# Moving the gelu derivatives of the first two chunks to fixed places in the order of a speech-joint kernel

## The chip, the cores and the metric

The kernel runs on one core of a Trainium2 chip. The metric is the device time of one execution in microseconds: the median of several runs for a verdict, and the hardware profiler's record of one execution for the reasons. The engines are TensorE (PE), VectorE (DVE), ScalarE (ACT), GpSimd (POOL) and SyncE (SP, used here for DMA issues only).

## The reference

Two strided convolutions, each followed by a tanh-gelu, feed a joint network; the kernel computes its output and all gradients.

```python
h = gelu(sum(xp[:, i:i+T] @ w1[i] for i in range(3)))[:, ::2]
f = gelu(sum(hp[:, i:i+T1] @ w2[i] for i in range(3)))[:, ::2]
j = tanh((f @ w_f)[:, :, None, :] + (g @ w_g)[:, None, :, :])
out = einsum("btud,dv->btuv", j, w_o)
```

x is (2, 16000, 256), g is (2, 8, 256), out is (2, 4000, 8, 256), everything in bfloat16. The eight results are `out` and the gradients of x, w1, w2, g, w_f, w_g and w_o for a given `grad_out`. The backward pass needs the derivative of each gelu at each position; that derivative work is what the change moves.

## The kernel before

**Tiling.** The 2 x 4000 output positions lie on one axis of 8016 columns (16 between the batches), cut into 16 chunks of 512 columns. A chunk's first convolution gives two tiles (even and odd positions, `par` 0 and 1) of 256 channels, its second convolution one. Channels lie on the 128 partitions in two halves, so a tile is 128x1024 elements.

**Stages of a chunk.** `conv_units` does the first convolution: PE writes `ps` (one of seven PSUM buffers), ACT copies it to `g_x`, `gelu` makes HT of it. `conv2_units` does the second one and its gelu gives FT. `fe_units` multiplies FT by w_f and ACT writes FE. `tanh` (ACT) makes JT for each of eight u. `joint_units` handles a pair of u: two products of grad_out with w_o's transpose (`gj`), evicted by DVE as NGZ with JSQ, the square of JT, as an operand; the output blocks (`o_block`, evicted by ACT); and the products for w_o's gradient (`gwo`, from JR, which is JT transposed). POOL adds the NGZ of all u into ACCN and the last time into NGFE. The backward pass of a chunk (`d1_units` makes GF from NGFE and G2; `row_units` turns tiles into rows; `d5_units` makes GH from GF and G1; then weight gradients and the gradient of x) runs during the next chunk's iteration.

**The gelu** (L248 on, called for each convolution tile) returns two lists of operations. `first`: ACT's Square into g_sq, a DVE scalar_tensor_tensor into g_s, ACT's Sigmoid in g_s, a DVE product into HT or FT. `second` is the derivative: five DVE operations, two tensor_scalar and three tensor_tensor, that end in G1 or G2. A chunk has three gelus. For chunk 0 each list is cut in two halves of 512 columns. The derivatives reuse the scratch tiles g_x, g_sq and g_s, which are free again only after them. Scratch comes from `gel` (three buffers of each name); for chunk 0's second convolution it comes from `rowp`, a pool of six tiles which `row_units` and `ghr_units` use later.

**The order.** The outer loop is over chunks. Iteration n weaves the joint of chunk n (the main generator) with a fill chain: the convolutions of chunk n + 1 and the backward pass of chunk n - 1. The main generator of chunk 0 yields 16 steps for each of four pairs of u, 64 in all (four `gj`, four transposes for JR, then output blocks and gwo); later chunks have 48. After each main step `weave` takes up to two operations from `later` (the `first` lists), one from `late` (the `second` lists) if it is open, and then a unit of the fill chain as often as a ratio allows: 0.4 for chunk 0 and 0.92 later. `late` opens when `conv2_units` of the next chunk has handed in its lists. Instructions are traced in this order, but the framework's scheduler then orders every engine's queue: an instruction traced late may be queued early if its operands are ready. `tc.keep_in_program_order` pins an instruction behind what was traced before it. Derivatives of chunks 2 and later are pinned (`pinned`), those of chunks 0 and 1 are not. In the profile the derivatives of chunks 0 and 1 carry L265, those of later chunks L268.

**Ahead of the loop** chunk 0's convolutions run with `warm` between them: matmuls on a zero tile `idle`, which is taken from the x pool (`xcp`, six tiles, four for a chunk).

Of the kernel before, what the change touches and what calls it, by code (L numbers as in the profile page):

```python
# [13 lines left out]
BF16 = mybir.dt.bfloat16  # L14
FP32 = mybir.dt.float32
ALU = mybir.AluOpType
# [4 lines left out]
GELU_A = float(2.0 * np.sqrt(2.0 / np.pi))  # L21

P = 128
KT = 2
# [4 lines left out]
CW = 512  # L29
# [3 lines left out]
def kernel(  # L33
# [22 lines left out]
    nc = tc.nc  # L56
    B, T, _ = x.shape
# [6 lines left out]
    def geom(n):  # L64
        c0 = n * CW
        return c0, min(CW, L - c0)
# [35 lines left out]
    xcp = pool("xcp", 6)  # L102
# [10 lines left out]
    rowp = pool("rowp", 6)  # L113
# [13 lines left out]
    def ps_f32():  # L127
        return psp.tile([P, 512], FP32, name="ps", tag="ps")
# [117 lines left out]
    def scratch(name, spare):  # L246
        if spare:
            return rowp.tile([P, 8, P], BF16, name="rows")[:].rearrange("p (k a) b -> p k (a b)", k=KT)  # L248
        return gel.tile([P, KT, CW], BF16, name=name)


    later, late = deque(), deque()
    late_open = [False]
    held = []
    NOSYNC = mybir.DependencyInfo(mybir.DependencyClass.NoSync, mybir.DependencyReason.DATA)

    def pump(k):
        for _ in range(k):
            if later:
                later.popleft()()  # L260

    def pump_late(k):
        for _ in range(k):
            if late and late_open[0]:
                late.popleft()()  # L265

    def pinned(op, n):
        return op if n <= 1 else (lambda: tc.keep_in_program_order(op()))  # L268

    def gelu(xb, W, h, gp, off, kts=((0, KT),), spare=False):  # L270

        sq, s = scratch("g_sq", spare), scratch("g_s", spare)
        TT, TS, STT = nc.vector.tensor_tensor, nc.vector.tensor_scalar, nc.vector.scalar_tensor_tensor
        first, second = [], []
        for (k0, k1) in kts:
            sq_, s_, x_ = sq[:, k0:k1, :W], s[:, k0:k1, :W], xb[:, k0:k1, :W]
            h_, gp_ = h[:, k0:k1, off:off + W], gp[:, k0:k1, off:off + W]
            first += [
                partial(nc.scalar.activation, out=sq_, in_=x_, func=ACT.Square, scale=GELU_R),
                partial(STT, out=s_, in0=sq_, scalar=1.0, in1=x_, op0=ALU.add, op1=ALU.mult),  # L280
                partial(nc.scalar.activation, out=s_, in_=s_, func=ACT.Sigmoid, scale=GELU_A),
                partial(TT, out=h_, in0=s_, in1=x_, op=ALU.mult),
            ]
            second += [
                partial(TS, out=sq_, in0=sq_, scalar1=3.0 * GELU_A, scalar2=GELU_A, op0=ALU.mult, op1=ALU.add),
                partial(TS, out=x_, in0=s_, scalar1=-1.0, scalar2=1.0, op0=ALU.mult, op1=ALU.add),
                partial(TT, out=sq_, in0=sq_, in1=x_, op=ALU.mult),
                partial(TT, out=sq_, in0=sq_, in1=h_, op=ALU.mult),
                partial(TT, out=gp_, in0=sq_, in1=s_, op=ALU.add),
            ]  # L290
        return first, second


    HALVES = ((0, 1), (1, 2))

    seconds0 = []
# [41 lines left out]
    def conv2_units(n):  # L338
        c0, W = geom(n)
        st = S[n]  # L340
        HT = st["HT"]
        if n > 0:
            pump(len(later))
        FT = ftp.tile([P, KT, CW], BF16, name="FT")
        G2 = ftp.tile([P, KT, CW], BF16, name="G2")
        st["FT"], st["G2"] = FT, G2
        if W % P:
            nc.gpsimd.memset(FT[:, :, W:W // P * P + P], 0.0)
        xb = scratch("g_x", n == 0)
        for mt in range(KT):  # L350
            ps = ps_f32()
            k = 0
            for (i, par, off) in ((1, 0, 2), (0, 1, 1), (2, 1, 2)):
                for kt in range(KT):
                    nc.tensor.matmul(ps[:, :W], lhsT=W2[:, i, kt, mt * P:(mt + 1) * P],  # L355
                                     rhs=HT[:, par, kt, off:off + W], start=(k == 0), stop=(k == 5))
                    k += 1
            nc.scalar.copy(out=xb[:, mt, :W], in_=ps[:, :W])
            yield
        first, second = gelu(xb, W, FT, G2, 0, HALVES if n == 0 else ((0, KT),), n == 0)  # L360
        if n == 0:
            for f in first:
                f()
        else:
            later.extend(first)
        late.extend(pinned(f, n) for f in second + seconds0)
        seconds0.clear()
        late_open[0] = True

    def fe_units(n):  # L370
        c0, W = geom(n)
        if n > 0:
            pump(len(later))
        FE = fep.tile([P, KT, CW], FP32, name="FE")
        S[n]["FE"] = FE
        for mt in range(KT):
            ps = ps_f32()
            for kt in range(KT):
                nc.tensor.matmul(ps[:, :W], lhsT=WF[:, kt, mt * P:(mt + 1) * P], rhs=S[n]["FT"][:, kt, :W],
                                 start=(kt == 0), stop=(kt == KT - 1))  # L380
            nc.scalar.copy(out=FE[:, mt, :W], in_=ps[:, :W])
            yield
# [351 lines left out]
    def chain(*gens):  # L734
        for gen in gens:
            yield from gen

    def empty(k):
        for _ in range(k):
            yield  # L740

    def weave(main, fill, ratio):

        due = 0.0
        for _ in main:
            pump(2)
            pump_late(1)
            due += ratio
            while due >= 1.0:
                due -= 1.0  # L750
                if next(fill, StopIteration) is StopIteration:
                    due = -1e9
# [7 lines left out]
    nc.sync.dma_start(out=W2[:], in_=w2.rearrange("i (kt p) n -> p i kt n", p=P))  # L760
    nc.sync.dma_start(out=WF[:], in_=w_f.rearrange("(kt p) n -> p kt n", p=P))
    nc.sync.dma_start(out=WO[:], in_=w_o.rearrange("(kt p) n -> p kt n", p=P))
    idle = xcp.tile([P, KT, CW + 16], BF16, name="XC")
    nc.vector.memset(idle[:], 0.0)
    small = const.tile([P, 1], FP32, name="small")
    nc.vector.memset(small[:], 0.0)
    nc.scalar.activation(out=small[:], in_=small[:], func=ACT.Sigmoid)
# [1 line left out]
    def warm(k):  # L769

        ps = ps_f32()
        for _ in range(k):
            tc.keep_in_program_order(nc.tensor.matmul(ps[:], lhsT=idle[:, 0, 0:P], rhs=idle[:, 0, 0:CW],
                                                      start=True, stop=True))
        yield

# [47 lines left out]
    for n in range(G):  # L824
        back, fwd = n > 0, n + 1 < G
        conv = conv_units(n + 1) if fwd else iter(())
        conv2 = conv2_units(n + 1) if fwd else iter(())
        late_open[0] = False
        parts = []
        if back:  # L830
            d1, e, rows, ghr = d1_units(n - 1), e_units(n - 1), row_units(n - 1), ghr_units(n - 1)
            parts += [islice(conv, 2), islice(d1, 1), islice(conv, 1), d1, conv, alternate(rows, d5_units(n - 1)),
                      gwf_units(n - 1), gw2_units(n - 1), islice(ghr, 1), islice(conv2, 1), ghr, conv2, islice(e, 6)]
            if fwd:
                parts.append(fe_units(n + 1))
            parts.append(e)
        else:
            parts += [conv, empty(3), islice(conv2, 1), empty(3), conv2, empty(3), fe_units(n + 1)]
        fill = chain(*parts)
        ratio = (0.92 if n > 0 else 0.4) if n + 1 < G else 0.72  # L840
        for up in range(U // 2):
            step = n * (U // 2) + up
            for i in range(2):
                if 2 * step + 4 + i < len(order):
                    load_got(*order[2 * step + 4 + i])
            if step + 1 < len(orderp):
                load_go(*orderp[step + 1])
            if up == 1:
                load_fr(n)
            if back and up < 2:  # L850
                load_xr(n - 1, 2 * up)
                load_xr(n - 1, 2 * up + 1)
            main = joint_units(n, up)
            weave(main, fill, ratio)
            if up == U // 2 - 1:
                for _ in fill:
                    pump(2)
                    pump_late(1)
                pump(len(later))
                late_open[0] = True  # L860
                pump_late(len(late))
            for i in range(2):
                if 2 * step + 2 + i < len(order):
                    tanh(*order[2 * step + 2 + i])
            if step + 1 < len(orderp):
                load_jr(*orderp[step + 1])
            if n + 2 < G:
                load_x(n + 2, ((0, 1, 3, 2)[up],))
    n = G - 1
# [30 lines left out]
    for b in range(B):  # L900
# [11 lines left out]
        for dt in range(KT):  # L912
            nc.tensor.matmul(GWG_ps[:, dt * D:(dt + 1) * D], lhsT=GR8[:, b, dt * P:(dt + 1) * P],
                             rhs=ngR[:].rearrange("u kt p -> u (kt p)"),
# [34 lines left out]
```

## Time and profile before

| what | value |
|---|---|
| median of the runs | 850.34 us (848.83 to 851.24, three runs) |
| profiled execution | 843.12 us |
| its span | 841.4 us |
| PE busy | 812.8 us (97%), mean granted clock 0.994 |
| DVE busy | 620.3 us (74%) |
| ACT busy | 678.4 us (81%) |
| POOL busy | 394.6 us (47%) |
| start (before FE of chunk 0) | 0 to 27.17 us |
| iteration of chunk 0 | 27.17 to 70.65 us |
| iteration of chunk 1 | 70.65 to 121.6 us |
| DMA moved | 187.21 MB, mean 223 GB/s |

The profiled execution is the record of one run, and its span is what lies between the first and the last instruction. A group's mean mixes contended and free executions: a 128x1024 tensor_scalar at L265 took 0.43 us at 38.9 us and 2.35 us at 49.29 us.

### The profile page before, as it was taken

What the parts mean: (1) busy time and instruction counts of PE and PEld (TensorE: products, weight loads), DVE (VectorE), ACT (ScalarE), POOL (GpSimd) and SP (SyncE); (2) the same over time, 40 slices, a digit from 0 to 9 for tenths busy, and PEclk for the clock granted to TensorE, in tenths of its full rate; (3) what the DMA queues carried; (4) which work ended last, traced back from release to release, by engine and by line L of the source; (5) the groups of instructions that cost most, each with busy time, mean ns of one, the idle gap of its engine ahead of it and who ended that gap; (6) DMA issues with size and microseconds to landing.
All of it is one profiled execution on the core that took longest, in us unless ns stands there. A gap on an engine that the chain in (4) does not pass through costs nothing.

```text
span 841.4 us, 17055 instructions
## 1 busy us (share of the span) xinstructions
PE 812.8 (97%) x6396; PEld 598.2 (71%) x6396; DVE 620.3 (74%) x1217; ACT 678.4 (81%) x1080; POOL 394.6 (47%) x423
## 2 busy tenths in 40 slices
PE   7969999999999999999999999999999999999997
PEld 3546677767768677676766777677686776878796
DVE  4896696876778767697866968768687676967644
ACT  3889998796978969699796987969789696987744
POOL 1154544444534535444486644445345354445661
PEclk9999999999999999999999999999999999999999
DMA  9988999999999999999999999999999999999954
GB/s 188 194 198 182 212 229 233 216 251 235 225 221 259 226 229 245 243 222 183 224 255 210 233 233 228 251 210 265 238 237 264 210 227 231 220 210 228 243 157 135
DMA packets 398515, 187.21 MB, mean 223 GB/s; under 512 B 346464, under 2 KB 382200, under 8 KB 398432
## 3 DMA queue, kind: packets, MB, share of 16 engines
q1 hardware_dynamic: 378112, 119.00, 77.9%
q0 software_dynamic: 20320, 67.12, 27.5%
q8 instruction: 50, 0.82, 0.4%
q14 instruction: 33, 0.27, 0.1%
HBM read 51.38 MB, written 50.34 MB: 121 GB/s over the span
## 4 chain that ended last, share of the span: by engine, by line
PE 43%; ACT 41%; DVE 6%; issue 5%; DMA 4%; POOL 0%; SPq 0%; ACTq 0%; POOLq 0%; DVEq 0%
ACT JT L396 12%; PE ps L593 7%; ACT OUT L692 6%; ACT JSQ L617 6%; PE GWO_ps L729 6%; PE ps L580 6%; PE ps L690 6%; ACT rows L462 5%; PE ps L355 5%; PE ps L524 4%; PE ps L623 4%; ACT g_s L260 3%; ACT g_x L323 3%; PE pst L460 2%; ACT GX L583 2%
## 5 line engine op out<-in xcount | busy, mean ns | idle before, releaser
L646 POOL TENSOR_TENSOR ACCN<-ACCN,NGZ 128x1024 f32<-128x1024 f32 (+1 forms) x80 | 168.7, 2109 | 69.1 <-DVE NGZ L627 68.0
L627 DVE SCALAR_TENSOR_TENSOR NGZ<-JSQ,ps 128x512 bf16<-128x512 bf16 (+3 forms) x272 | 167.5, 640 | 43.2 <-PE ps L623 39.9
L692 ACT CAST OUT<-ps 128x512 bf16<-128x512 f32 (+1 forms) x252 | 148.4, 600 | 58.4 <-PE ps L690 58.2
L396 ACT ACTIVATE JT<-FE,GE 128x512 bf16<-128x512 f32 (+3 forms) x272 | 182.3, 711 | 4.0 <-PE ps L623 1.9
L617 ACT ACTIVATE JSQ<-JT 128x1024 bf16<-128x1024 bf16 (+1 forms) x128 | 135.8, 1064 | 25.6 <-DVE NGZ L627 25.6
L729 PE MATMUL GWO_ps<-GO,JR 128*128 128x256 bf16 (+1 forms) x1008 | 148.6, 273 | 2.1 <-DVE JR L462 2.1
L690 PE MATMUL ps<-WO,JT 128*128 128x256 bf16 (+1 forms) x1008 | 148.7, 274 | 0.3 <-ACT rows L462 0.3
L717 POOL DMA_DIRECT2D out_dram<-OUT x76 | 55.8, 735 | 184.4 <-ACT OUT L692 171.5
L623 PE MATMUL ps<-GOT,WOT 128*128 128x512 bf16 (+1 forms) x512 | 139.2, 376 | 0.8 <-DVE rows L462 0.8
L260 DVE SCALAR_TENSOR_TENSOR g_s<-g_sq,g_x 128x1024 bf16<-128x1024 bf16 (+2 forms) x49 | 81.2, 1657 | 50.1 <-ACT g_sq L260 50.1
L729 PEld LDWEIGHTS <-JR 128*128 128x128 bf16 (+1 forms) x1008 | 96.9, 98 | 28.6 <-DVE JR L462 2.4
L690 PEld LDWEIGHTS <-JT 128*128 128x128 bf16 (+1 forms) x1008 | 97.9, 98 | 22.1 <-issue 1.6
L580 PE MATMUL ps<-W1T,GH 128*128 128x256 bf16 (+2 forms) x756 | 100.4, 273 | 0.0
L408 DVE TENSOR_TENSOR ACC<-ACC,ps 128x512 f32<-128x512 f32 x90 | 61.5, 684 | 44.5 <-PE ps L524 32.8
L580 PEld LDWEIGHTS <-GH 128*128 128x128 bf16 (+2 forms) x756 | 83.5, 116 | 13.0
L320 PE MATMUL ps<-XC,W 128*128 128x512 bf16 (+1 forms) x384 | 91.3, 375 | 1.1 <-DMA XC<-in_x_dram 1.1
L593 PE MATMUL ps<-rows,XR 128*128 128x256 bf16 (+1 forms) x756 | 90.4, 273 | 0.0
L593 PEld LDWEIGHTS <-XR 128*128 128x128 bf16 (+1 forms) x756 | 74.0, 98 | 11.6
L583 ACT CAST GX<-ps 128x512 bf16<-128x512 f32 (+2 forms) x126 | 72.2, 587 | 10.5 <-DMA out_dram<-GX 4.1
L241 POOL DMA_DIRECT2D out_dram<-GX x67 | 36.7, 548 | 82.1 <-ACT GX L583 75.0
L623 PEld LDWEIGHTS <-WOT 128*128 128x128 bf16 x512 | 48.5, 98 | 33.6 <-issue 2.3
L320 PEld LDWEIGHTS <-W 128*128 128x128 bf16 x384 | 37.4, 98 | 38.5 <-issue 1.4
(131 smaller groups left out, 1214.2 us busy)
## 6 DMA issues: line engine op xcount, KB each, us to landing
GO<-in_grad_out_dram SPq DMA_DIRECT2D x56, 512.0 KB, 5.3
out_dram<-OUT POOLq DMA_DIRECT2D x56, 512.0 KB, 5.5
out_dram<-GX POOLq DMA_DIRECT2D x55, 256.0 KB, 4.3
XR<-in_x_dram POOLq DMA_DIRECT2D x39, 256.0 KB, 6.3
XR<-in_x_dram POOLq DMA_DIRECT2D x13, 320.0 KB, 6.2
GOT<-in_grad_out_dram SPq DMA_TRANSPOSE x136, 5.7
JR<-JT SPq DMA_TRANSPOSE x128, 4.8
GO<-in_grad_out_dram SPq DMA_DIRECT2D x4, 384.0 KB, 5.0
```

Source lines behind the costliest of these rows:

```text
L260: later.popleft()()
L320: nc.tensor.matmul(ps[:, :W], lhsT=W1[:, i, kt, mt * P:(mt + 1) * P], rhs=st["X", c][:, kt, 16 + sh:16 + sh + W], start=(k == 0), stop=(k ...
L396: nc.scalar.activation(out=JT[:, mt, lo:hi], in_=S[n]["FE"][:, mt, lo:hi], func=ACT.Tanh, bias=GE[:, b, mt, u:u + 1], scale=1.0)
L580: nc.tensor.matmul(ps[:M, cj * D:(cj + 1) * D], lhsT=GH[:, par, kt, o:o + s * (M - 1) + 1:s], rhs=W1T[:, i, kt, :], start=(j == 0), stop=( ...
L593: nc.tensor.matmul(ps[:, dt * D:(dt + 1) * D], lhsT=XR[:M, 4 * k + i + 2 * (1 - par), dt * P:(dt + 1) * P], rhs=t[:M, g + 2 * par:g + 2 * ...
L617: nc.scalar.activation(out=JSQ[:, :, :W], in_=JT[:, :, :W], func=ACT.Square)
L623: nc.tensor.matmul(ps[:, :W], lhsT=WOT[:, kt, mt * P:(mt + 1) * P], rhs=GOT[:, kt, :W], start=(kt == 0), stop=(kt == KT - 1))
L627: nc.vector.scalar_tensor_tensor(out=NGZ[:, mt, lo:hi], in0=JSQ[:, mt, lo:hi], scalar=1.0, in1=ps[:, lo:hi], op0=ALU.subtract, op1=ALU.mul ...
L646: st["last"] = nc.gpsimd.tensor_tensor(out=out, in0=in0, in1=st["NGZ", u][:, :, :W], op=ALU.add)
L690: nc.tensor.matmul(ps[:M, j * V:(j + 1) * V], lhsT=st["JT", u][:, kt, o:o + M], rhs=WO[:, kt, :], start=(kt == 0), stop=(kt == KT - 1))
L692: nc.scalar.copy(out=OUT[:M, k, :], in_=ps[:M, :])
L729: nc.tensor.matmul(GWO_ps[:, dt, :], lhsT=JR[:M, j, dt, k, :], rhs=GO[:M, k, j * V:(j + 1) * V], start=(n_gwo[0] == 0), stop=(n_gwo[0] == ...
```

## The change

- A third queue, `slow`, with a budget `slow_open` that begins at 5. `weave` takes at most one operation from it at each main step while the budget lasts (`pump_slow`). Derivatives of chunks 0 and 1 go there, in the order first convolution (both parities), then second convolution; later chunks use `late` as before.
- `pinned` pins every derivative, also those of chunks 0 and 1.
- Derivatives of chunk 0 are whole (128x1024) and no longer in halves: 15 operations in place of 30. With chunk 1's 16 (one is a POOL copy) `slow` holds 31: five are taken in the first steps of chunk 0's iteration; `opened(15)`, placed in the fill chain one unit after chunk 1's second convolution, allows 15 more; the last 11 are taken in the first steps of chunk 1's iteration.
- The scratch of chunk 1's second convolution also comes from the row tiles.
- `idle` is taken from the row tiles, not from the x pool.

```diff
-    later, late = deque(), deque()
-    late_open = [False]
+    later, late, slow = deque(), deque(), deque()
+    late_open, slow_open = [False], [5]
...
+    def pump_slow(k):
+        for _ in range(min(k, slow_open[0], len(slow))):
+            slow_open[0] -= 1
+            slow.popleft()()
+
     def pinned(op, n):
-        return op if n <= 1 else (lambda: tc.keep_in_program_order(op()))
+        return lambda: tc.keep_in_program_order(op())
...
-            second += [
-                partial(TS, out=sq_, in0=sq_, scalar1=3.0 * GELU_A, scalar2=GELU_A, op0=ALU.mult, op1=ALU.add),
...
-            ]
+        sq_, s_, x_, h_, gp_ = sq[:, :, :W], s[:, :, :W], xb[:, :, :W], h[:, :, off:off + W], gp[:, :, off:off + W]
+        second += [
+            partial(TS, out=sq_, in0=sq_, scalar1=3.0 * GELU_A, scalar2=GELU_A, op0=ALU.mult, op1=ALU.add),
+            partial(TS, out=x_, in0=s_, scalar1=-1.0, scalar2=1.0, op0=ALU.mult, op1=ALU.add),
+            partial(TT, out=sq_, in0=sq_, in1=x_, op=ALU.mult),
+            partial(TT, out=sq_, in0=sq_, in1=h_, op=ALU.mult),
+            partial(TT, out=gp_, in0=sq_, in1=s_, op=ALU.add),
+        ]
...
-        xb = scratch("g_x", n == 0)
+        xb = scratch("g_x", n <= 1)
...
-        first, second = gelu(xb, W, FT, G2, 0, HALVES if n == 0 else ((0, KT),), n == 0)
+        first, second = gelu(xb, W, FT, G2, 0, HALVES if n == 0 else ((0, KT),), n <= 1)
...
-        late.extend(pinned(f, n) for f in second + seconds0)
+        (late if n > 1 else slow).extend(pinned(f, n) for f in (second + seconds0 if n > 1 else seconds0 + second))
         seconds0.clear()
-        late_open[0] = True
+        late_open[0] = n > 1
...
+    rate = [1]
+
+    def opened(k):
+        slow_open[0] += k
+        return
+        yield
...
             pump_late(1)
+            pump_slow(rate[0])
...
-    idle = xcp.tile([P, KT, CW + 16], BF16, name="XC")
-    nc.vector.memset(idle[:], 0.0)
+    idle = rowp.tile([P, 8, P], BF16, name="rows")[:].rearrange("p a b -> p (a b)")
+    nc.vector.memset(idle, 0.0)
...
-            parts += [conv, empty(3), islice(conv2, 1), empty(3), conv2, empty(3), fe_units(n + 1)]
+            parts += [conv, empty(3), islice(conv2, 1), empty(3), conv2, empty(1), opened(15), empty(2), fe_units(n + 1)]
...
                 pump_late(len(late))
+                if n == 0:
+                    pump_slow(len(slow))
+                    slow_open[0] = len(slow)
```

More of the change, by code (lines that the diff above doesn't have):

```diff
@@ L283, in gelu @@
             ]
-            second += [
-                partial(TS, out=sq_, in0=sq_, scalar1=3.0 * GELU_A, scalar2=GELU_A, op0=ALU.mult, op1=ALU.add),
[L286 to L289, printed above, removed]
-            ]
+        sq_, s_, x_, h_, gp_ = sq[:, :, :W], s[:, :, :W], xb[:, :, :W], h[:, :, off:off + W], gp[:, :, off:off + W]
[6 more added lines that the diff above has]
+        ]
         return first, second
@@ L772, in warm @@
         for _ in range(k):
-            tc.keep_in_program_order(nc.tensor.matmul(ps[:], lhsT=idle[:, 0, 0:P], rhs=idle[:, 0, 0:CW],
+            tc.keep_in_program_order(nc.tensor.matmul(ps[:], lhsT=idle[:, 0:P], rhs=idle[:, 0:CW],
                                                       start=True, stop=True))
```

## The prediction

> **What bounds the kernel now.** I read first the busy time of each engine by stretch: the start (to 27.17), chunk 0's iteration (to 70.65), the first half of the next one, and for comparison a whole steady iteration. Columns: the stretch, its length, busy time with instruction count for PE, PE's weight loads, DVE, ACT, POOL, then PE's granted clock, DMA share, GB/s.
>
> ```profile
> 27.17:70.65 43.48, 36.05 (x253) 22.43 (x252) 38.31 (x81) 37.83 (x58) 16.62 (x12) 0.92 0.80 181
> 70.65:92.00 21.35, 20.80 (x150) 13.01 (x147) 14.41 (x28) 20.78 (x32) 13.62 (x17) 1.00 1.06 221
> ...
> 121.60:172.30 50.70, 50.05 (x396) 36.95 (x394) 38.27 (x70) 42.34 (x67) 23.11 (x24) 1.00 1.12 236
> ```
>
> From 70.65 on PE is at 97 to 99% and at full clock: what PE loses after that is lost for good. Only chunk 0's iteration has slack: PE idles 7.4 of 43.5 us and part of the rest runs at a low clock, while DVE (38.3) and ACT (37.8) are nearly full. The second view is the order of work there, on DVE, then ACT and PE (start, duration, engine, line, operation, tiles, idle time before with what ended it).
>
> ```profile
> 36.49 2.37 DVE L260 SCALAR_TENSOR_TENSOR g_s<-g_sq,g_x 128x1024 bf16<-128x1024 bf16 x1
> ...
> 48.61 0.76 DVE L265 TENSOR_SCALAR g_sq<-g_sq 128x1024 bf16<-128x1024 bf16 x1
> 49.29 2.35 DVE L265 TENSOR_SCALAR g_x<-g_s 128x1024 bf16<-128x1024 bf16 x1
> 51.67 0.69 DVE L265 TENSOR_TENSOR g_sq<-g_sq,g_x 128x1024 bf16<-128x1024 bf16 x1
> ...
> 56.83 2.23 DVE L260 SCALAR_TENSOR_TENSOR g_s<-g_sq,g_x 128x1024 bf16<-128x1024 bf16 x1
> ...
> 61.25 0.68 DVE L260 TENSOR_TENSOR FT<-g_s,g_x 128x1024 bf16<-128x1024 bf16 x1
> ...
> 66.54 0.69 DVE L627 SCALAR_TENSOR_TENSOR NGZ<-JSQ,ps 128x512 bf16<-128x512 bf16 x1 [1.98 <-PE ps L623]
> ```
>
> ```profile
> 53.56 1.08 ACT L260 ACTIVATE g_sq<-g_x 128x1024 bf16<-128x1024 bf16 x1
> ```
>
> ```profile
> 54.21 0.38 PE L460 MATMUL pst<-ident,JT 128*128 128x128 bf16 x4 [1.55 <-DVE JR L462]
> ...
> 59.45 1.05 PE L729 MATMUL GWO_ps<-GO,JR 128*128 128x256 bf16 x8 [2.13 <-DVE JR L462]
> 61.98 1.01 PE L379 MATMUL ps<-FT,WF 128*128 128x512 bf16 x2 [1.48 <-DVE FT L260]
> ```
>
> Derivative work (L265) sits ahead of the second chunk's second gelu: its square is ready at 54.64, its next DVE step starts at 56.83. FT comes at 61.93 and PE waits for DVE three times, 5.2 us. After it PE runs slowly:
>
> ```profile
> 60.00:62.00 2.00, 0.52 (x6) 0.31 (x4) 1.97 (x3) 1.71 (x3) 1.04 (x1) 0.60 0.13 34
> 62.00:64.00 2.00, 2.00 (x7) 0.97 (x7) 1.90 (x4) 0.71 (x2) 0.00 (x0) 0.50 0.68 237
> 64.00:66.00 2.00, 2.00 (x8) 1.03 (x7) 0.56 (x1) 1.46 (x3) 0.00 (x0) 0.50 0.00 0
> ```
>
> Half clock (0.50) from about 61 to 67: some 3 us of PE work.
>
> **Part 1, the start.** Before, 30 half-size derivatives of chunk 0 run between 13.0 and 30.8 us; 22 begin before 27.8, mostly while DVE has nothing else. Three of them stand in the queue before the last HT piece (0.29 + 0.54 = 0.83 us in the chain of waits). Taking them out gives at most 0.83, but ACT is busy without a gap from 11.04 to 17.38 and fixes that piece too: between -0.8 and 0. The idle tile leaves the XC buffers, so one x load needs no release; PE's wait for XC at 31.44 is 1.08 us: between -1.1 and 0. I take -0.6 for both. What is lost: these 30 (12 x 0.29 + 18 x 0.41 = 10.9 us) cost almost nothing there, and now lie in later stretches.
>
> **Part 2, five pinned operations in steps 1 to 5 of chunk 0's iteration.** Full-size spacing from the rows: scalar form 0.46, tensor form 0.73, so one set of five is 2 x 0.46 + 3 x 0.73 = 3.1 us. They now stand between the NGZ evictions and the first JR copies, and behind them the g_s step of 36.49. NGZ begins about 32.0; 4 x 0.61 + 4 x 0.35 + 3.1 ends near 38.5, so g_s starts 2 us later; it took 2.37 because POOL's add ran beside it (1.22 in the next one), so it ends at 39.7 against 38.86. ACT, full from 27.8 to 54.64 but for 0.75 us, waits for it: +0.8 (bounds 0 and +2).
>
> **Part 3, up to FT.** Chunk 1's ten derivatives ahead of 54.6 (2.9 + 5.2 = 8.1 us, port waits in them) go. They are worth little up to the square at 54.64, which ACT's full queue sets (54.64 + 0.8 - 0.6 = 54.84). From there: g_s 2.2, sigmoid 1.06, product 0.68: FT at 58.8, 3.1 earlier than 61.93.
>
> **Part 4, fifteen pinned operations in steps 38 to 52.** The fill is served in steps 3, 5, 8, 10, 13 and 15 of each sixteen, which puts the release in step 37. Steps 38 to 52 give PE little (0.4 to 0.5 us each) and DVE one derivative each, with chunk 0's last JR copies and NGZ evictions behind them. NGZ of step 49 comes after FT + 3 JR copies (1.05) + 11 derivatives (2 x 3.1 + 0.46 = 6.6) + port waits. Beside a POOL add a scalar form took 1.68 and 2.35 instead of 0.43; of the two adds in that stretch I charge 1.2 (bounds 0 and 3.8). 58.8 + 8.9 = 67.7, against 66.54: +1.1. The last of the four NGZ, three more derivatives between, ends near 72.0 (69.8 before), JR near 74.1 (70.53). PE has seven PSUM buffers; four hold step 49 to 52's products until NGZ frees them, so PE stands from about 63 to 68 and the o blocks end near 71.5 against 70.65: **+0.9**. Bounds: -4 if PE follows FT without a stall (3.1 and the half clock), +3 if the stall throttles PE again (1.75 us of o blocks at half clock, plus the higher port wait).
>
> The Trainium skill, "SBUF — State Buffer" (Who interferes with whom), says that DVE and GpSimd lock the shared port for a whole instruction. The rows agree for operations with all their operands in SBUF (2.35 against 0.43). By it the two adds could cost 2 x 2.1 = 4.2 instead of 1.2, and the sum below would be +6.1 by that figure.
>
> **Part 5, eleven operations in steps 1 to 11 of the second iteration.** Ten on DVE (2 x 3.1 = 6.2) and one 0.19 us copy on POOL, where only adds and output DMAs queue. DVE idles 6.9 of 21.35 us there, but the ten fall in the first 12 us, together with NGZ, GF, g_s, HT and GH. GF's second half ended at 79.81; the seven DVE operations to there (73.24 to 79.81 less 0.8 idle, 5.8) and five derivatives (3.1), begun at 74.1, end at 83.0, and PE needs it at 81.05, by then 81.95: **+1.0**. At step 11 DVE is still 3.7 us behind (6.2 + 0.9 less 3.4 of idle), and the NGZ evictions of 86 to 90 hold PSUM: I take **+1.2**. Together bounds 0 (all in the idle time) and +6.7.
>
> **Row tiles.** Chunk 1's scratch holds three of six until step 11; the rows units from step 8 use the other three up to the fourth tile in step 12. At nothing if DVE is on time, else part of the +6.7.
>
> **Sum.** +0.9 (with -0.6, +0.8 and FT's -3.1 in it) + 1.0 + 1.2 = +3.1 us against the profiled execution: 843.12 (span 841.4 and 1.7 around it) becomes 846.2. The runs' median is 850.34, 7.2 above; with the same difference 853.4.
>
> **Rivals.**
> (a) **Faster**: FT's 3 to 5 us are kept, because the built order lets PE fill its wait with outer work and PE stays at full clock: 5.2 of waits and 3 of half clock less 3 given back in the second iteration: -5, 845.3. For it: PE's losses really stand behind FT. Against: DVE's work in chunk 0's iteration stays the same (before 8.1 + 4.2 = 12.3 us of derivatives after 30.8, now 20 x 0.62 = 12.4).
> (b) **No change**: FT's gain pays for the tail (+0.9 becomes 0), and DVE's 6.9 us of idle take the ten: 850.3. For it: those idle rows; against: they come in pieces of 0.5 to 2.7 us, half of them after step 11.
> (c) **Much slower**: DVE's backlog meets the row tiles. If op 26 is late by 3.7 us, the fourth rows tile, ACT's in-order copy into it and everything behind wait: 3.1 + 3.7 = +6.8, 857.1. It decides only if DVE is behind at step 12.
> (d) **The clock falls again**: PE stands 5 us from 63 to 68 (part 4), as much as the three waits that ended in half clock before (5.2 us); the o blocks (1.75 us) then take twice as long: 853.4 + 1.75 = 855.2. Against: those waits came in a stretch of ten us, this one may be filled with outer products. The Trainium skill, "TensorE: Matmul & The Clock Gate" (What's actually happening), has PE fall to half rate after an idle window of about 3.4 us, which speaks for it; the 0.50 rows agree in direction.
>
> **Chances.** Forecast 0.28, (d) 0.10, (c) 0.12, (b) 0.22, (a) 0.28. About 0.3% (2.55 us) can be told from no change: slower 0.47 (forecast, (c), (d), less a little of the forecast that falls short of 2.55), same 0.25 (that and most of (b)), faster 0.28 (most of (a), a little of (b)). The likeliest's own range is 850 to 857; to hold 8 in 10 it takes (b), most of (a) and (c): 845 to 858.5.
>
> **What would show it.** Right: FT near 58.8; no L265 work before 32; NGZ of up 3 at 67 to 70 with a PE wait on DVE in front; GF's second half after 82; PE idle time in 70 to 92 above 2 us (now 0.55). Wrong: FT later than 61 (the pin holds up something on ACT), or NGZ of up 3 earlier than 66 with PE at full clock from 60 on (rival a), or second-iteration derivatives all inside DVE's idle time (b).

## The result, and the profile after

The change makes the kernel slower. In 22 runs of each, the changed kernel's median is 851.71 us (844.22 to 868.86) against 846.8 us (840.73 to 858.08) before; the ratio is 1.0065, 95% interval 1.0041 to 1.0089, so +3.5 to +7.5 us. A second comparison of the two gave 1.0058, 1.0029 to 1.0087. Runs more than 1.5% above the fastest of their kernel are called slow and left out of the ratios; the first profile after the change is of such a run (856.96 us), so two more follow, the last of them of a fast run (847.88 us).

Where the time goes can be read more sharply from marks in the profiles than from whole runs. Four marks serve: FE of chunk 0 (the start is over), the end of FT of chunk 1, the first product of chunk 1's iteration on PE, and NGFE of chunk 1 on POOL, near that iteration's end. The start itself shifts by up to 0.8 us from run to run with the landing of g (DVE's first copy behind it lies between 7.7 and 8.5 us), so the last column is counted from that copy.

| us | FE of chunk 0 | FT of chunk 1 | chunk 1's iteration | NGFE of chunk 1 | same, from the first copy |
|---|---|---|---|---|---|
| before | 27.17 | 61.93 | 70.65 | 119.29 | 110.83 |
| after | 26.02 | 59.37 | 72.98 | 122.84 | 114.69 |

From chunk 2 on the order of every engine's queue is the same in both kernels, and from NGFE of chunk 1 to that of chunk 2 it takes 50.8 us in both. So the front of the kernel, the first seventh, loses 3.6 to 3.9 us, and FT is earlier, as the change wants it, while what follows is later. The next view is DVE's timeline of the changed kernel (start, duration, engine, line, operation, tiles; derivatives of chunks 0 and 1 are now at L273).

```profile
53.28 2.23 DVE L260 SCALAR_TENSOR_TENSOR rows<-rows 128x1024 bf16<-128x1024 bf16 x1
55.43 2.34 DVE L273 TENSOR_SCALAR g_sq<-g_sq 128x1024 bf16<-128x1024 bf16 x1
57.69 0.41 DVE L468 COPY JR<-pst 128x512 bf16<-128x512 bf16 x1
58.03 0.41 DVE L273 TENSOR_SCALAR g_x<-g_s 128x1024 bf16<-128x1024 bf16 x1
58.36 0.41 DVE L468 COPY JR<-pst 128x512 bf16<-128x512 bf16 x1
58.70 0.67 DVE L260 TENSOR_TENSOR FT<-rows 128x1024 bf16<-128x1024 bf16 x1
...
64.10 0.69 DVE L633 SCALAR_TENSOR_TENSOR NGZ<-JSQ,ps 128x512 bf16<-128x512 bf16 x1 [2.00 <-ACT OUT L698]
...
66.25 0.68 DVE L633 SCALAR_TENSOR_TENSOR NGZ<-JSQ,ps 128x512 bf16<-128x512 bf16 x1
...
66.86 0.69 DVE L273 TENSOR_TENSOR G<-rows 128x1024 bf16<-128x1024 bf16 x1
67.46 2.35 DVE L273 TENSOR_SCALAR g_sq<-g_sq 128x1024 bf16<-128x1024 bf16 x1
69.73 0.68 DVE L633 SCALAR_TENSOR_TENSOR NGZ<-JSQ,ps 128x512 bf16<-128x512 bf16 x1
...
70.33 0.68 DVE L273 TENSOR_TENSOR g_sq<-g_sq,g_x 128x1024 bf16<-128x1024 bf16 x1
70.94 0.67 DVE L633 SCALAR_TENSOR_TENSOR NGZ<-JSQ,ps 128x512 bf16<-128x512 bf16 x1
```

Two things are to be seen. A derivative that took 2.34 us (0.41 is what the same form takes two lines below) stands ahead of two JR copies and of FT: the pin did not hold it behind FT. And the four NGZ evictions of the last pair of u are spread over 64.1 to 71.6 with derivatives between them. Before, they ran one behind the other from 66.54 to 69.2; the last of them:

```profile
68.51 0.68 DVE L627 SCALAR_TENSOR_TENSOR NGZ<-JSQ,ps 128x512 bf16<-128x512 bf16 x1
```

PE's timeline of the changed kernel shows who waits (in brackets: idle time before, and what ended it):

```profile
58.16 1.89 PE L735 MATMUL GWO_ps<-GO,JR 128*128 128x256 bf16 x8 [4.23 <-DVE JR L468]
...
67.00 0.60 PE L696 MATMUL ps<-WO,JT 128*128 128x256 bf16 x4 [0.85 <-DVE NGZ L633]
70.47 2.72 PE L696 MATMUL ps<-WO,JT 128*128 128x256 bf16 x12 [2.87 <-DVE NGZ L633]
```

The three waits of before (1.55, 2.13, 1.48) became 4.23, 0.85 and 2.87. The last twelve output products of 70.47 took 2.72 us, at half clock (0.57 granted in 70 to 72 and 72 to 74); twelve of them took 1.47 us at 47.14 in the kernel before. By stretch (chunk 0's iteration but for its first 1.0 us, first half of chunk 1's; columns as in the prediction):

```profile
27.00:72.98 45.98, 37.07 (x250) 23.00 (x248) 36.27 (x71) 39.32 (x60) 17.96 (x11) 0.90 0.81 187
72.98:94.00 21.02, 19.79 (x134) 11.72 (x133) 20.50 (x39) 19.49 (x30) 11.65 (x16) 0.98 0.96 172
```

From FE on, chunk 0's iteration is 47.0 us long (43.5), with 8.9 us of idle PE (7.4). In the second row DVE is busy 20.50 of 21.02 us where it had 14.41 of 21.35, and PE loses 1.2 us there (0.55).

### The profile page after: what moved, and what is told of

Read it like the earlier page. It is cut to its first block, busy times and chain, and to the rows that moved or that the text cites. A ratio compares the mean times of both kernels' runs of the same rounds, so it can differ in the third digit from the quotient of the medians.

```text
span 855.1 us, 17044 instructions
## 1 busy us (share of the span) xinstructions
PE 818.6 (96%) x6396; PEld 599.5 (70%) x6396; DVE 621.8 (73%) x1202; ACT 678.9 (79%) x1080; POOL 397.8 (47%) x423
## 4 chain that ended last, share of the span: by engine, by line
PE 43%; ACT 39%; DMA 7%; issue 5%; DVE 5%; POOL 0%; SPq 0%; ACTq 0%; POOLq 0%
ACT JT L402 12%; PE GWO_ps L735 7%; PE ps L599 6%; ACT OUT L698 6%; PE ps L696 6%; DMA JR<-JT 6%; ACT JSQ L623 6%; PE ps L586 5%; ACT rows L468 5%; PE ps L530 4%; PE ps L361 4%; PE ps L629 4%; ACT g_s L260 3%; PE pst L466 2%; ACT g_x L329 2%
## 5 line engine op out<-in xcount | busy, mean ns | idle before, releaser
L735 PE MATMUL GWO_ps<-GO,JR 128*128 128x256 bf16 (+1 forms) x1008 | 150.5, 275 | 9.9 <-DMA JR<-JT 5.4
L260 DVE SCALAR_TENSOR_TENSOR g_s<-g_sq,g_x 128x1024 bf16<-128x1024 bf16 (+2 forms) x48 | 78.4, 1635 | 54.2 <-ACT g_sq L260 54.1
L326 PEld LDWEIGHTS <-W 128*128 128x128 bf16 x384 | 37.7, 98 | 38.9 <-issue 2.0
```

The lines of the kernel that those rows point to most:

```text
L326: nc.tensor.matmul(ps[:, :W], lhsT=W1[:, i, kt, mt * P:(mt + 1) * P], rhs=st["X", c][:, kt, 16 + sh:16 + sh + W], start=(k == 0), stop=(k ...
L735: nc.tensor.matmul(GWO_ps[:, dt, :], lhsT=JR[:M, j, dt, k, :], rhs=GO[:M, k, j * V:(j + 1) * V], start=(n_gwo[0] == 0), stop=(n_gwo[0] == ...
```

## The experiments

Two theories stood against each other. AMOUNT: what costs is derivative work in stretches where DVE is full; chunk 0's share was free at the start. ORDER: what costs is that the pins put a derivative, with its wait for POOL's port, ahead of the JR copies and FT. In the expectations "chunk 1's iteration" and NGFE are the marks of the table. All marks of all runs stand in the table behind the last experiment.

**Chunk 0's derivatives back at the start, chunk 1's sixteen all in chunk 0's iteration** (on the changed kernel).

```diff
+        if n == 0:
+            for f in second + seconds0:
+                f()
+        else:
+            (late if n > 1 else slow).extend(...)
...
-    late_open, slow_open = [False], [5]
+    late_open, slow_open = [False], [0]
...
-opened(15)
+opened(16)
```

The derivatives of chunk 0 are also in halves again.

> Chunk 0's thirty half-size derivatives go back to where before had them (free to run at the start); chunk 1's sixteen are all taken after its second convolution, none in the second iteration. Theory AMOUNT (what costs is derivative work in stretches where DVE is full; chunk 0's was free at the start): the tail of chunk 0's iteration is as full as after the change (16 against 15), so chunk 1's iteration begins on PE at 71.5 to 73 (before 70.65, after 72.98), but nothing is pushed into it: NGFE of chunk 1 at 119.5 to 121 (before 119.29, after 122.84). Theory ORDER (what costs is that the pins put a derivative and two port waits ahead of the JR copies and of FT): the order there is the same as after the change, so NGFE of chunk 1 stays at 122 or later.

Chunk 1's iteration began at 72.83, NGFE came at 121.79, between the two: the tail is as late as after the change and only the second iteration is freed. From its first product to NGFE it took 48.96 us, like before (48.64), against 49.86 after the change: the second iteration costs 1.2 us more with the eleven operations, and 0.9 of it goes with them. Half clock reached further into the iteration here (0.50 granted from 72 to 74 us and 0.54 from 74 to 76; 0.57 and 1.00 after the change), so this pair alone does not price the eleven; the next kernel has them at full clock and takes 49.51 us, 0.9 more than before. The whole was still slower than before: 1.0071 (1.0013 to 1.0128).

**The same with five and eleven** (`opened(5)`).

> As c0_free_16, but five of chunk 1's sixteen behind its second convolution and eleven in the second iteration. AMOUNT: ten fewer derivatives in the tail than after the change, so chunk 1's iteration begins at 67 to 70 (before 70.65), and with about +2 us in the second iteration NGFE of chunk 1 comes at 117.5 to 119.5: total 0 to 2 us below before. ORDER: the first derivative still stands ahead of two JR copies and of FT, so chunk 1's iteration begins at 72 or later and NGFE at 121.5 or later: total 2 us or more above before.

67.97 and 117.48: AMOUNT holds here, 4.9 us less at the end of chunk 0's iteration than with sixteen, for eleven operations fewer in the tail (ten on DVE), although the first one still stands ahead of FT. The ratio, 1.000 (0.9958 to 1.0043), is too wide to show the 1.8 us of the marks.

**One more DVE operation behind each of the fifteen.**

```diff
             slow.popleft()()
+            if extra[0]:
+                tc.keep_in_program_order(nc.vector.tensor_scalar(out=WGT[:], in0=WGT[:], scalar1=1.0, scalar2=0.0, op0=ALU.mult, op1=ALU.add))
```

> The changed kernel with one more DVE operation (tensor_scalar on a 128x512 tile that nobody needs until the end, 0.20 to 0.29 us) behind each of the fifteen pinned ones: 3.0 to 4.3 us of DVE work more, nothing else. AMOUNT: DVE is the limit of that stretch, so chunk 1's iteration begins 2.5 to 4.3 us later than after the change (75.5 to 77.3), and NGFE of chunk 1 is as much later. ORDER: DVE has room behind FT, so less than 1 us.

The iteration began at 74.06, +1.1, and NGFE came at 123.81, +1.0: a third of the 3.0 us of work, near what ORDER says. DVE's timeline of this kernel:

```profile
65.79 0.42 DVE L276 TENSOR_SCALAR g_sq<-g_sq 128x1024 bf16<-128x1024 bf16 x1
...
68.68 2.22 DVE L273 TENSOR_SCALAR WGT<-WGT 128x512 bf16<-128x512 bf16 x1
...
73.44 2.21 DVE L273 TENSOR_SCALAR WGT<-WGT 128x512 bf16<-128x512 bf16 x1
```

The derivative that took 2.35 at 67.46 is done in 0.42 here, and a small operation two derivatives later (0.28 elsewhere) takes the wait for POOL instead: whatever comes beside the add waits for it. That saves nothing, since there are as many long operations as in the changed kernel (2.22 and 2.21 us here, 2.35 at 67.46 and 2.27 at 72.48 there). What is saved is idle time: in the changed kernel DVE stood 2.00 us before the NGZ of 64.10, in this one it is busy without a gap from 50.4 to 77 us. The fifteen (at 0.20 us each, 3.0 in all) filled these 2.0, and the other 1.0 delayed what follows. AMOUNT is too simple: DVE is not the limit of the whole stretch.

**The fifteen really behind FT.**

```diff
-            later.extend(first)
+            later.extend(first[:-1])
+            later.append(lambda: ft_done.append(first[-1]()))
...
-            slow.popleft()()
+            op = slow.popleft()()
+            if len(ft_done) == 1:
+                tc.add_manual_dep(op.ins, ft_done[0].ins.name, NOSYNC, reason="behind FT")
```

> The changed kernel with the fifteen really behind FT's product (an order edge more for each): no derivative ahead of FT and of the last JR copies. ORDER: PE's wait of 4.23 us for JR shrinks by about 2 and the clock stays up; chunk 1's iteration begins at 71 or earlier, NGFE of chunk 1 at 120.8 or earlier. AMOUNT: the same fifteen only come later, the NGZ of the last pair as late as now: chunk 1's iteration begins at 72 to 73, NGFE at 122 to 123.

70.36 and 120.43: ORDER holds in both marks. DVE and PE of this kernel:

```profile
55.43 0.74 DVE L472 COPY JR<-pst 128x512 bf16<-128x512 bf16 x2
56.63 1.42 DVE L375 TENSOR_TENSOR FT<-rows 128x1024 bf16<-128x1024 bf16 x1 [0.46 <-ACT rows L261]
57.96 0.41 DVE L276 TENSOR_SCALAR g_sq<-g_sq 128x1024 bf16<-128x1024 bf16 x1
```

```profile
55.90 1.55 PE L739 MATMUL GWO_ps<-GO,JR 128*128 128x256 bf16 x8 [1.97 <-DVE JR L472]
...
58.09 1.01 PE L389 MATMUL ps<-FT,WF 128*128 128x512 bf16 x2 [0.64 <-DVE FT L375]
...
67.84 2.72 PE L700 MATMUL ps<-WO,JT 128*128 128x256 bf16 x12 [2.87 <-DVE NGZ L637]
```

The JR copies and FT come right behind g_s, PE's first wait falls from 4.23 to 1.97, and 2.4 us of the loss are gone (2.3 by the last column). The last wait, 2.87 for NGZ, and the half clock behind it stay, with derivatives between the NGZ as in the changed kernel. The clock did not stay up, though ORDER expected it: 0.57 and 0.58 were granted from 56 to 58 and 58 to 60, behind the wait of 1.97. So both theories hold a part.

**The idle tile alone**, on the kernel before.

> The kernel before with only the idle tile taken from the row tiles. If the start gained 1.15 us (FE of chunk 0 at 26.02 instead of 27.17) by the freed x buffer, FE moves here too, to 26.0 to 26.3. If it gained by the derivatives that left the start, FE stays at 27.0 to 27.2. PE's wait of 1.08 us for XC at 31.44 goes in both (0 to 0.2). NGFE of chunk 1 at 118 to 119.3 (before 119.29).

FE came at 26.81; counted from the first copy (8.09) it is 18.72, and 18.71 in before (27.17 less 8.46): unchanged. In the changed kernel it is 17.87. The 0.84 us of the start are the derivatives' doing. PE's wait for XC is gone, and NGFE is 0.55 us earlier by the last column of the table, less than the spread of three profiles of the changed kernel there (114.04 to 114.87): a gain from the tile is not shown.

**Without POOL's adds of u = 2 to 6 in chunk 0**, on the changed kernel and, later, on the one before.

```diff
-        if u == 0:
+        if u == 0 or n == 0 and 1 < u < U - 1:
             return
```

> The changed kernel without POOL's adds of u = 2 to 6 in chunk 0 (so chunk 0's part of the gradients behind NGFE lacks them), which takes the port waits out of chunk 0's iteration and no work from DVE. In the changed kernel's rows three derivatives and two g_s steps took 2.2 to 2.35 us instead of 0.4 to 1.2. If port waits are a main part of the loss: chunk 1's iteration begins at 68.5 to 71 (after the change 72.98) and the 2.3 us derivative ahead of FT takes 0.45. If the loss is the number of derivatives and their order alone: 72 to 73.

> The kernel before without the same POOL adds (chunk 0's part of the gradients behind NGFE lacks them). In before, two g_s steps and two derivatives waited on the port, some 5 us. If the change's loss is mostly more waiting on the port: NGFE of chunk 1 at 114.5 to 116.5, as late as in no_adds (115.89), so that the change costs under 1 us without the adds. If amount and order cost as much without port waits: 112 to 113, and the change costs 3 to 4 us here too.

```profile
52.79 1.22 DVE L260 SCALAR_TENSOR_TENSOR rows<-rows 128x1024 bf16<-128x1024 bf16 x1
53.93 0.42 DVE L273 TENSOR_SCALAR g_sq<-g_sq 128x1024 bf16<-128x1024 bf16 x1
...
62.07 0.42 DVE L273 TENSOR_SCALAR g_sq<-g_sq 128x1024 bf16<-128x1024 bf16 x1
```

The lines are of the changed kernel without the adds, and these are the operations of 53.28, 55.43 and 67.46 above, at 1.22, 0.42 and 0.42 us. (The other 2.3 us entry for g_s in the changed kernel's timeline, at 38.67, is two steps of 1.2 each.) Chunk 1's iteration began at 64.80 there, earlier than the 68.5 to 71 expected. The changed kernel gains 6.5 us by the last column, the one before 5.4. So waiting for the port is a large cost of both kernels, but the difference is only 1.1 us; without the adds the change costs 2.8 us instead of 3.9. That lies between the two cases expected of the second run. The 1.1 us come from single profiles, and the adds of u = 1 and 7 stay: beside the last one a derivative of the changed kernel still takes 2.29 us at 65.15, where before has none. So 1.1 us is a rough size of the change's part.

**Both findings in one kernel**: chunk 0's derivatives free at the start, but ordered behind the last transposed weight copy; chunk 1's behind FT, ten or five of them in chunk 0's iteration. The edges behind FT are those of above, `slow_open` begins at 0, and `trans` holds the copies of the transposed weights.

```diff
+            for f in second + seconds0:
+                tc.add_manual_dep(f().ins, trans[-1].ins.name, NOSYNC, reason="behind the transposes")
```

> Built from both findings: chunk 0's derivatives free at the start but behind the last transposed weight copy, chunk 1's pinned really behind FT's product, ten in chunk 0's iteration and six in the second one. AMOUNT plus ORDER: FE of chunk 0 at 26.0 to 26.3, FT of chunk 1 by 58.5, chunk 1's iteration from 64.5 to 67.5 (before 70.65), NGFE of chunk 1 at 113.5 to 116.5 (119.29): 3 to 6 us below before, ratio 0.993 to 0.997. If derivatives at the start cost there after all: FE at 27 or later and NGFE of chunk 1 at 117 or later.

> As best_10 with five in chunk 0's iteration and eleven in the second one. Chunk 1's iteration begins up to 1 us earlier than in best_10 or as early (if DVE has room behind FT), the second iteration takes 0.7 to 1.2 us more: NGFE of chunk 1 at 114 to 117, ratio 0.993 to 0.998.

> best_5 once more, unedited, for a narrower ratio. From the marks (NGFE of chunk 1 3.9 us before that of the kernel before): ratio 0.993 to 0.998; if the gain is taken back by the transfers later in the kernel, 0.999 or more.

By the marks they do nearly what was expected: FE at 26.08 and 25.94, chunk 1's iteration from 67.29 and 65.85, NGFE at 115.44 and 115.39, 3.5 us below before by the last column. In whole runs ten gave 1.000 (0.9961 to 1.004), which shows no gain; five gave 0.9983 (0.9947 to 1.0018), and 0.9925 (0.989 to 0.996) the second time. Each measured against before, the version with five lies clearly below the changed kernel. It beats before by some tenths of a per cent: the second comparison shows it, the first does not. Chunk 0's iteration (but for its first 1.1 us) and what follows, by stretch, in the version with five:

```profile
27.00:65.85 38.85, 34.50 (x249) 21.86 (x248) 30.03 (x71) 36.34 (x57) 16.27 (x10) 0.96 0.91 196
65.85:87.00 21.15, 19.55 (x139) 11.96 (x137) 18.37 (x37) 20.11 (x31) 12.89 (x15) 1.00 1.09 193
```

The iteration is 39.9 us long from FE on (47.0 in the changed kernel), with 4.3 us of idle PE in place of 8.9 and the clock at 0.96; the second row still pays 1.6 us of idle PE for the eleven.

**The changed kernel again**, twice.

> The changed kernel once more, unedited. NGFE of chunk 1 at 122.5 to 123.2 (122.84 in the first profile), and from there to the NGFE of chunk 15 690 to 695 us, as in before (692.4); the 702.1 of the first profile is not the change's if this holds.

> The changed kernel unedited, for a second ratio and a third profile. If the loss is what the marks show (3.5 to 3.9 us by NGFE of chunk 1) and nothing more: ratio 1.003 to 1.006, and NGFE of chunk 8 to NGFE of chunk 9 at 50 to 53 us (50.5 in before, 56.4 and 58.0 in two profiles of the changed kernel). If the changed kernel loses 6 to 7 us there in every execution: again 56 to 58, and ratio 1.009 or more.

NGFE of chunk 1 came at 123.08 and 122.39, so the front's loss repeats. From there to NGFE of chunk 15 it took 698.7 and 694.3 us (702.1 in the first profile, 692.4 in before), the former above the 690 to 695 expected. From chunk 8's NGFE to chunk 9's it took 56.4 and 51.9 us (58.0 in the first profile, 50.5 in before, 53.0 in the kernel with only the idle tile moved). In the first two profiles ACT waited there for JR's transfers:

```profile
ACT JT L402 <- DMA JR<-JT: 9.6, 4, 4.4
```

(from the list of waits of the whole first profile: in total, times, longest; 7.3 us of it lie between 470 and 545 us). It is not in every execution of the changed kernel, and kernels without the change have some of it: over all kernels here the stretch from chunk 1's NGFE to chunk 15's took 691.2 to 710.5 us, the longest in the one with only the idle tile moved, whose single execution took 860.15 us with a front as short as before's. So a single execution's time does not rank these kernels. Whether the wait comes more often with the change stays open; the front alone, 3.9 us in the median of three profiles or 0.46% (3.2 to 4.0), is inside both intervals of the ratio, near the lower end of the first.

| us | FT of chunk 1 | chunk 1's iteration | NGFE of chunk 1 | from the first copy |
|---|---|---|---|---|
| before | 61.93 | 70.65 | 119.29 | 110.83 |
| after (three profiles) | 59.37, 59.46, 59.59 | 72.98, 73.22, 72.53 | 122.84, 123.08, 122.39 | 114.69, 114.87, 114.04 |
| chunk 0 at the start, 16 | 60.33 | 72.83 | 121.79 | 113.38 |
| chunk 0 at the start, 5 + 11 | 60.43 | 67.97 | 117.48 | 109.08 |
| fifteen operations more | 59.63 | 74.06 | 123.81 | 115.55 |
| behind FT | 58.05 | 70.36 | 120.43 | 112.37 |
| idle tile alone | 60.82 | 69.72 | 118.37 | 110.28 |
| no adds, changed | 56.07 | 64.80 | 115.89 | 108.18 |
| no adds, before | 58.53 | 64.68 | 113.58 | 105.42 |
| both findings, 10 + 6 | 58.15 | 67.29 | 115.44 | 107.32 |
| both findings, 5 + 11 | 58.02, 57.69 | 65.85, 65.24 | 115.39, 114.80 | 107.27, 107.08 |

## Why the prediction was right, and where it was not

**Direction and size.** Forecast +3.1 us, measured +3.6 by NGFE of chunk 1, +3.9 by the last column (+3.2 and +4.0 in the other two profiles), and +0.65% (0.41 to 0.89) over whole runs, where the forecast had 0.37%; on the 850.34 of the forecast that is 855.9, inside the range of 850 to 857. The main statement, that derivatives which cost little at the start were moved to where DVE is in everybody's way, is shown by the kernels that put chunk 0's back: 1.3 us less with the tail as full as after the change (114.69 to 113.38), 5.6 with five in the tail (109.08).

**The start** (-0.6): -0.84, and the experiments name the part: the derivatives in the queue, not the x buffer, for which no gain is shown.

**Steps 1 to 5** (+0.8 on ACT): the first g_s ended near 39.9, and I had put it at 39.7 (the terms of its start add up to 38.9, not 38.5). The port wait went to the fifth derivative (2.28 us at 35.80), not to g_s. But ACT was not held up:

```profile
39.91 1.06 ACT L260 ACTIVATE g_s<-g_s 128x1024 bf16<-128x1024 bf16 x1 [0.24 <-DVE g_s L260]
...
51.61 1.08 ACT L260 ACTIVATE rows<-rows 128x1024 bf16<-128x1024 bf16 x1
```

It waited 0.24 us there (0.41 at 38.90 before), and its square of the second convolution began 25.6 us behind FE, against 26.4 before. So the +0.8 did not come; ACT was 0.8 us earlier instead.

**FT** (58.8): 59.37, and that they are so close is luck. The square was ready at 52.69, not at 54.84, and g_s ended at 55.5, not at 57.0; what followed was about 2 us longer than the forecast's sigmoid and product. The step assumed that all fifteen stay behind FT. They did not: `keep_in_program_order` ties an operation to the one traced just before it on its engine, here a JR copy, not to all that was traced earlier, and FT's product, waiting for ACT, could be overtaken. The kernel with a real order has FT at 58.05. This is the step of the working that failed: the wait put on PE from 63 to 68 really came in parts, 4.23 us for JR ahead of FT, and 0.85 and 2.87 for NGZ at 67.00 and 70.47.

**The tail** (+0.9): +2.3, the term that was most under-sized. I charged 1.2 us for the port; the derivatives of 55.43 and 67.46 alone waited 1.9 us each, 3.9 together, just above the upper bound of 3.8. And rival (d) came true on top: the clock fell again, and the twelve products of 70.47 cost 1.25 us more than at full clock (1.75 estimated for sixteen). The last NGZ came at 71.6, near what was worked out (72.0; the 69.8 of before should be 69.2); the first came earlier (64.10, not 67.7), since the built order put more derivatives behind it.

**The second iteration** (+2.2): 49.86 us from first product to NGFE against 48.64, so +1.2. The eleven cost 0.9 of it at full clock (49.51 with five and eleven); the rest may be the four first products, still at half clock (1.39 us against 1.03), which no run shows apart. GF's second half ended at 84.32, later even than the 83.0 expected, but PE waited for it only 0.25 us, and 0.21 for NGZ: it was itself 2.7 us late by then. Two errors of opposite sign, +1.4 in the tail and -1.0 here, nearly cancel in the sum (+3.55 by the raw marks against +3.1): the direction was earned, the closeness of the sum was luck. Of the signs named in advance GF's came, but PE's idle time from 70 to 92 us was 1.0 us and not above 2, and the first NGZ of the last pair came at 64.10, outside 67 to 70.

**Rivals.** (a) fell: even with the order that the change only meant to make (the kernel behind FT) the front is 1.5 us longer than before by the last column; -3.5 us came only with chunk 0's derivatives back at the start as well. (b) fell: DVE's idle time in chunk 1's first 21 us was used up (20.50 busy) and PE lost by it. (c) fell: between 73 and 95 us the list of waits has one on rows, PE's 0.7 us for ACT's copy, and before had 0.69 for the same copies.

**Port and clock.** The Trainium skill, "SBUF — State Buffer" (Who interferes with whom), was right against my smaller charge: an exclusive lock for the whole instruction. With the adds out, 2.34 became 0.42. For the clock, the Trainium skill, "TensorE: Matmul & The Clock Gate" (What's actually happening) has an idle window of about 3.4 us; here the clock fell after one wait of 4.23 us (0.50 granted from 58 to 60), which agrees, but in before it fell after three waits of 1.55, 2.13 and 1.48 us in pieces, in the changed kernel a second time after waits of 0.85 and 2.87, and in the kernel behind FT after one of 1.97. How much idle time in pieces is enough, no run here shows.

## What to carry to other kernels

Ask of work that is moved off a critical step what it cost where it was: here it was almost free (0.84 us) in DVE's idle time at the start, and in the tail it stood among the evictions that free PSUM buffers. More work costs what does not fit into the engine's idle time: 3.0 us of it, put where DVE had 2.0 idle, cost 1.1. Check in the built order of the engine that a pin holds what it is meant to hold; an edge to one neighbour lets later-traced work run ahead of an operation that is not ready. And where one engine's long instructions lock another out, count one full wait for each of them that meets the moved work.

## What was not expected of the hardware

A 2.1 us POOL add and DVE operations with all operands in SBUF exclude each other to the end of the add (0.41 to 2.34 us), whichever operation meets it: a 0.28 us one took 2.22. NGZ evictions, with one operand in PSUM, took 0.68 us beside an add as without one (at 52.67 in the changed kernel, the add from 52.30 on). And half clock came also without any single PE wait above 2.2 us: 0.50 granted from 62 to 66 in the kernel before.
